# Two of a macro group's last sums move to GpSimd, eleven others and the words of the third product start later

## The chip, the cores and the metric

The kernel runs on one core of one Trainium2 chip, in one launch. The metric is the device time in microseconds, the median of several executions. TensorE is called PE in the profile, VectorE DVE, ScalarE ACT, GpSimd POOL and SyncE SP.

## The reference

The input is a sequence of 2048 rows of 576 numbers. It is normalised row by row; the result goes through a linear-attention block with 32 heads and through a gated feed-forward block, and the two are joined.

```
xn = layernorm(x)
q, k, v = split(xn @ wqkv)                      # 32 heads of 18
s = linear_attention(phi(q), phi(k), v) @ wo
h = gelu(xn @ w_gate) * (xn @ w_up)             # 2048 x 4608
out = x + s * silu(h @ w_down)                  # h @ w_down: 2048 x 576
```

All inputs and outputs are float32.

## The kernel before

Every large product is made in fp32r passes: an operand is cut into a high word (ScalarE copies it to fp32r) and a low word (VectorE subtracts the high word from the source), and TensorE multiplies high by high, high by low and low by high. `split`, `cut` and `make_words` are such pairs of one ScalarE and one VectorE instruction.

The attention part comes first, then 36 matrices of the feed-forward's gate and up projections (`gate_matrix`, `up_matrix`), and last the down projection (`down_all`). The hidden values are kept transposed, 4608 x 2048, and both of these dimensions are split in four, so that one group of values is sixteen blocks of 128 x 512 numbers. Nine such groups (`NM = 9`, called macro groups, m = 0 to 8) make up the whole. The down projection multiplies not the sixteen blocks but fixed sums and differences of them, in 26 products (`PROD`) in place of more. Which sums are needed is written out by hand: `ADDS` lists 28 sums as (name, first operand, second operand, sign, due hook). `ADDS_LAST` is the list for the last macro group. The 26 values that products read (`FORM`) are written to DRAM tensors `hs` (one for each macro group) by `put_out`, 128 x 512 numbers each, and read back for each product by `load_unit`.

**Due hooks.** A matrix has seven hooks, a macro group 28 (`HOOKS`). Hook numbers of group m start at 28 m. `run_events` runs what is due at a hook. For the last group, hooks 0 to 27 lie in the feed-forward, and from hook 28 on in the down projection: there, an event due at hook 28 + n is run in the first step (p, k) in which half the count of contraction tiles done, 9 p + 2 k, has reached n. `add_up` gives a sum to POOL, unless it belongs to the last group and is due after hook 28: then it goes to VectorE. The comparison is

```
late = m == NM - 1 and at > HOOKS * NM
```

so that a last-group sum due at exactly 28 is made by POOL. The same flag says whether a sum may be written over an operand that is still to be put out. The put-outs of the last group are issued on POOL's queue, those of the others on SP's.

**The down projection.** A product p has nine contraction tiles, one for each macro group, taken in five steps k = 0 to 4 (`UNITS`): two tiles in each of the first four, one in the last. A tile is 12 matmuls (four banks, three passes), so a product is 108. In step (p, k) the program order is: the sums that are due; loads of `w_down` (`load_reg`); `change` (VectorE adds and subtracts blocks of `w_down`) or `make_words` (the two words of the next product's weight block: c = 0 is `w_head` or `w_first`, tiles 0 to 4; c = 1 is `w_end`, tiles 5 to 8); `cut(u + 2)`, the cut of the values of the step two further on; the matmuls; the loads of the values of product p + 1 for the same step, into the buffers just read; in step 1 the banks of the product before are read.

Buffers for raw values (`raw_a`, `raw_b`, from product 4 on `raw_h`, `raw_g`) hold the value, and then its low word; `hi` and a part of `beside` hold high words in three places taken in turn. So ScalarE's half of a cut waits until TensorE has finished the step three back, and a load until the buffer is read. Sums and gate values of the last groups live in the buffers `spot_h`, `spot_m` and `spot_g`; `spot_h` becomes `raw_h` later. Products 1 and 23 use the words of the products before them (`SHARED = {1: 0, 23: 22}`), so that in steps 2 and 3 of product 0 the words made are those of product 2.

The engines' instructions are pinned in program order (`tc.keep_in_program_order`); a semaphore wait stops all that follows on the same engine. In the profile every VectorE instruction has line L125, every ScalarE one L122, POOL's sums L131, DMA issues L134, and the down projection's matmuls L128.

Of the kernel before, what the change touches and what calls it, by code (L numbers as in the profile page):

```python
# [62 lines left out]


ADDS_LAST = ADDS[:14] + (
# [4 lines left out]
)  # L70

FORM = (33, 18, 11, 19, 31, 27, 29, 15, 30, 25, 6, 43, 40, 42, 35, 17, 4, 26, 39, 24, 41, 22,
# [18 lines left out]
def block_kernel(ctx, tc, x, xe, wq_d, wkv_d, wo, wgu_d, wd_d, out):  # L91
# [29 lines left out]
    def act(*args, **kw):  # L121
        pin(nc.scalar.activation(*args, **kw))  # L122

    def vec(op, *args, **kw):
        pin(getattr(nc.vector, op)(*args, **kw))  # L125
# [286 lines left out]
    def run(todo, n=None):  # L412
        for _ in range(len(todo) if n is None else min(n, len(todo))):
            todo.pop(0)()
# [438 lines left out]
    def run_events(at):  # L853
        for f in events.pop(at, []):
            f()
# [53 lines left out]
    SHARED = {1: 0, 23: 22}  # L909
    reg, acc_t, banks, raw_v, hi_v, word, early = {}, {}, {}, {}, {}, {}, {}  # L910

    def load_reg(at, nm, third=None):
        if at not in reg:
            b = big(REG[at], [P, REG_W], F32, f"b_{at}")
            reg[at] = b[:, 0 : KT * HALF].rearrange("p (k d) -> p k d", k=KT)
        j, c = int(nm[0]) - 1, int(nm[1]) - 1
        par, f = divmod(KP[j], 2)
        src = wd_d[par::2, :, f, c * HALF : (c + 1) * HALF].rearrange("g p d -> p g d")
        k = slice(0, KT) if third is None else slice(3 * third, 3 * third + 3)
        dma(out=reg[at][:, k], in_=src[:, k])  # L920
# [18 lines left out]
    def load_unit(p, k):  # L939
        if p >= NP:  # L940
            return
        raw_v[p, k] = v = raw_place(p, k)
        for i in range(*UNITS[k]):
            dma(out=v[:, i - UNITS[k][0]].bitcast(F32), in_=hs_d[i][:, PROD[p][0]])
# [13 lines left out]
    def cut(u):  # L958
        p, k = divmod(u, NU)
        if p >= NP:  # L960
            return
        hi, lo = hi_place(p, k), raw_v[p, k]
        hi_v[p, k] = hi
        src = lo.bitcast(F32)
        act(hi, src, AF.Copy)
        vec("tensor_sub", lo, src, hi.bitcast(F32))
# [3 lines left out]
    def word_tiles(p):  # L970
        if p not in word:
            n = len(word)
            b = n % 2
            t = ring(("end", b), lambda: big((11, 4)[b], [P, 2, 4, HALF], F32R, f"w_end{b}"))
            end = [t[:, i] for i in range(2)]
            if b == 0:
                head = [
                    ring(("head", i), lambda i=i: mid(i, [P, 5, HALF], F32R, f"w_head{i}"))
                    for i in (0, 2)
                ]  # L980
            else:
                head = [
                    beside()[:, 2 * TBN : 2 * TBN + 5 * HALF].rearrange("p (k d) -> p k d", k=5),
                    big(12, [P, 5, HALF], F32R, "w_first") if n == 1
                    else ring(("head", 1), lambda: mid(1, [P, 5, HALF], F32R, "w_head1")),
                ]
            word[p] = [[v[i] for v in (head, end)] for i in range(2)]
        return word[p]
# [24 lines left out]
    def change(p, c):  # L1013
        for nm, a, op, b in CHANGES.get(p, ()):
            r = [reg[x][:, HALVES[c]] for x in (nm, a, b)]
            vec("tensor_add" if op == "+" else "tensor_sub", *r)
# [3 lines left out]
    def make_words(p, c):  # L1020

        if p >= NP or p in SHARED or (p, c) in made:
            return
        made.add((p, c))
        hi, lo = (w[c] for w in word_tiles(p))
        src = reg[FROM[p]][:, HALVES[c]]
        if PROD[p][2]:
            act(hi, src, AF.Copy, scale=-1.0)
            vec(
                "scalar_tensor_tensor", lo, src, -1.0, hi.bitcast(F32),  # L1030
                op0=ALU.mult, op1=ALU.subtract,
            )
        else:
            act(hi, src, AF.Copy)
            vec("tensor_sub", lo, src, hi.bitcast(F32))

    def down_mm(p, kt, js):
        if p < 2 and p not in banks:
            banks[p] = [
                (own_bank if p == 0 and i < 2 else bank)(f"bd_{p}_{i}") for i in range(TT)  # L1040
            ]
        c = int(kt > 4)
        hi, lo = (w[c][:, kt - 5 * c] for w in word[SHARED.get(p, p)])
        k = kt // 2
        h = [v[p, k][:, kt % 2] for v in (hi_v, raw_v)]
        for j in js:
            for i, (a, w) in enumerate(((0, hi), (0, lo), (1, hi))):
                mm(
                    banks[p % 2][j][:, 0:HALF], h[a][:, j * P : (j + 1) * P], w,
                    start=(PROD[p][1] == 1 and kt == 0 and i == 0),  # L1050
                    stop=(kt == KT - 1 and i == 2), skip_group_check=True,
                )
# [9 lines left out]
    def read(p, js=range(TT)):  # L1062
        for o, d in PROD[p][3]:
            a = acc_of(o)
            for j in js:
                src = banks[p % 2][j][:, 0:HALF]
                if (o, j) not in begun:
                    begun.add((o, j))
                    act(a[:, j], src, AF.Copy)
                else:  # L1070
                    vec("tensor_add" if d > 0 else "tensor_sub", a[:, j], a[:, j], src)
# [15 lines left out]
    def load_sx(o):  # L1087
        tb, cols, rows = places(o)
        if o in SX:
            sx = big(SX[o], [P, 2, TT, HALF], F32, f"sx_{o}")  # L1090
            all_ = slice(tb * TBN, (tb + 1) * TBN)
            dma(out=sx[:, 0], in_=s_d[tb][:, :, cols])
            dma(out=sx[:, 1], in_=x[all_, cols].rearrange("(t p) d -> p t d", p=P))
            sxs[o] = [sx[:, :, j] for j in range(TT)]
        else:
            sxs[o] = [tmp([P, 2, HALF], f"sx_{o}_{j}") for j in range(TT)]
            for j, t in enumerate(sxs[o]):
                dma(out=t[:, 0], in_=s_d[tb][:, j, cols])
                dma(out=t[:, 1], in_=x[rows(j), cols])
# [3 lines left out]
    def close(o, j):  # L1103
        _, cols, rows = places(o)
        y, t = acc_of(o)[:, j], sxs[o][j]
        act(y, y, AF.Silu, scale=float(SIGN[o]))
        vec("tensor_mul", t[:, 0], y, t[:, 0])
        vec("tensor_add", t[:, 0], t[:, 0], t[:, 1])
        stores.append(lambda: dma(out=out[rows(j), cols], in_=t[:, 0]))
# [40 lines left out]
    def down_all():  # L1150
        late = []
        last = NP - 1
        for u in range(NP * NU):
            p, k = divmod(u, NU)
            n = KT * p + 2 * k
            for at in sorted(events):
                if at <= H_END + n // 2:
                    run_events(at)
            if p in LOADS and k < 3:
                load_reg(*LOADS[p], k)  # L1160
            if k == 0:
                for o, e in ENDS.items():
                    if e == p:
                        load_sx(o)
            if k < 2:
                change(p + 1, k)
            elif k < 4:
                make_words(p + 2 if p + 1 in SHARED else p + 1, k - 2)
            cut(u + 2)
            if p == last and k == 2:  # L1170
                break
            for kt in range(*UNITS[k]):
                down_mm(p, kt, range(TT))
            load_unit(p + 1, k)
            run(stores)
            if k == 1 and p:
                read(p - 1)
                late += [
                    lambda o=o, j=j: close(o, j) for o, e in ENDS.items() if e == p - 1
                    for j in range(TT)  # L1180
                ]
            else:
                run(late, 2)
        run(late)
        run(stores)
        o = next(o for o, e in ENDS.items() if e == last)
        for j in range(TT):
            for kt in range(UNITS[2][0], KT):
                down_mm(last, kt, (j,))
            late += close_last(o, j, last, 2 if j == TT - 1 else 1)  # L1190
            run(late, len(late) - 1)
        run(late)
# [205 lines left out]
    for q in range(NQ):  # L1398
# [9 lines left out]
        for i in range(7):  # L1408
            todo[i].append(lambda at=7 * q + i: run_events(at))
        (gate_matrix if q % 2 == 0 else up_matrix)(g, todo)  # L1410
    down_all()


# [47 lines left out]
```

## Time and profile before

| | |
|---|---|
| median of 3 runs | 1488.77 us (1488.16 to 1489.85) |
| the profiled execution's own time | 1488.81 us |
| its span, first to last instruction | 1487.1 us |
| granted TensorE clock, mean | 0.998 |
| PE / DVE / ACT / POOL busy | 1471.1 / 1145.7 / 560.1 / 581.0 us |
| the down projection's first matmul | at 1103.93 us |

Rows of instructions in order of time read: start in us, length in us, engine, line, operation, output <- input, shape, count, and in brackets the idle time of the engine before it and what ended it. The names are those of the program's tiles without buffer numbers; a sum is a row with `spot_` on both sides, a cut one with `raw_` and `hi` or `beside`. Rows of a table by stretches read: the stretch, its length, the busy time of each engine with its number of instructions, the granted clock, the DMA engines' busy share, and what they moved. PE rows overlap, since matmuls are pipelined.

### The profile page before, as it was taken

The page shows a single profiled execution, that of the slowest core. Times are in us where ns is not written, and L with a number is a line of the kernel's source. Part 1 is how long each engine was busy: PE and PEld are TensorE (multiplying, and loading weights), DVE is VectorE, ACT ScalarE, POOL GpSimd, SP SyncE. Part 2 cuts the span into 40 slices and gives each one's busy share as a digit, 9 for nine tenths or more (in the row PEclk, how much of TensorE's full clock was granted, in tenths as well). Part 3 has the DMA queues.
Part 4 walks back from the last instruction along what each step waited for, and adds up shares of the span by engine and source line. Part 5 has one row for each costly group of instructions (what it writes and reads, how often), then busy time and mean ns, then how long its engine had stood idle before and what let it go on. Part 6 is the DMA issues. An engine that isn't in the chain of part 4 may idle for free.

```text
span 1487.1 us, 21863 instructions
## 1 busy us (share of the span) xinstructions
PE 1471.1 (99%) x8128; PEld 1310.2 (88%) x8128; DVE 1145.7 (77%) x1587; ACT 560.1 (38%) x923; POOL 581.0 (39%) x515
## 2 busy tenths in 40 slices
PE   8999999999999999999999999999999999999998
PEld 8989988988888888888888888888889999999998
DVE  7567466557787788787878787788787988989887
ACT  5434335433223322323322223322234546455454
POOL 4342241124656757555675655757641000000000
PEclk9999999999999999999999999999999999999999
DMA  4425003452231522433242232422379888767886
GB/s 163 176 117 213 6 2 136 167 207 86 92 128 54 181 85 93 149 106 110 82 163 101 98 128 67 167 86 98 129 274 314 262 258 261 240 188 239 272 291 214
DMA packets 115132, 230.62 MB, mean 155 GB/s; under 512 B 10882, under 2 KB 42882, under 8 KB 112978
## 3 DMA queue, kind: packets, MB, share of 16 engines
q1 hardware_dynamic: 112370, 217.17, 43.5%
q0 software_dynamic: 2656, 12.06, 2.2%
q8 instruction: 64, 1.05, 0.3%
q14 instruction: 42, 0.34, 0.1%
HBM read 146.57 MB, written 82.58 MB: 154 GB/s over the span
## 4 chain that ended last, share of the span: by engine, by line
PE 95%; DVE 2%; DMA 1%; issue 1%; ACT 0%; SPq 0%; POOL 0%; DVEq 0%; POOLq 0%; ACTq 0%
PE bd L128 24%; PE ga L746 15%; PE de L746 15%; PE al L746 15%; PE kv L128 8%; PE be L746 7%; PE q L128 4%; PE s L128 4%; PE kv_a L128 1%; PE xt L205 1%; PE d L128 1%; DMA raw<-in_wgu_dram 0%; DVE wb L125 0%; DMA raw_b<-hs 0%; PE kw L128 0%
## 5 line engine op out<-in xcount | busy, mean ns | idle before, releaser
L131 POOL TENSOR_TENSOR sm<-raw 128x384 f32<-128x384 f32 x72 | 76.7, 1065 | 154.6 <-DMA raw<-in_wgu_dram 129.0
L128 PE MATMUL kv<-wkv,xo_B 128*128 128x384 f32 x672 | 127.6, 346 | 0.3 <-ACT xo_B L122 0.3
L125 DVE TENSOR_TENSOR wa<-sm,wa 128x768 fp32r<-128x768 f32 x72 | 93.0, 1291 | 36.1 <-ACT wa L122 35.3
L128 PEld LDWEIGHTS kv<-wkv,xo_B 128*128 128x128 f32 x672 | 119.4, 193 | 1.2 <-ACT xo_B L122 0.8
L128 PE MATMUL bd<-w_head,hi 128*128 128x288 f32 x516 | 118.0, 294 | 0.0
L125 DVE TENSOR_TENSOR wb<-raw,wb 128x256 fp32r<-128x256 f32 (+1 forms) x108 | 108.0, 1000 | 7.3 <-ACT wb L122 5.8
L125 DVE TENSOR_TENSOR wa<-raw,wa 128x256 fp32r<-128x256 f32 x72 | 64.8, 900 | 50.7 <-ACT wa L122 47.5
L122 ACT ACTIVATE hi<-raw_h 128x1024 fp32r<-128x1024 f32 x59 | 62.4, 1060 | 96.8 <-PE bd L128 64.0
L128 PE MATMUL bd<-w_end,hi 128*128 128x288 f32 x448 | 89.9, 294 | 0.0
L122 ACT ACTIVATE spot_h<-spot_h 128x512 f32<-128x512 f32 x49 | 30.8, 633 | 151.7 <-DVE spot_h L125 151.7
L125 DVE TENSOR_TENSOR raw_h<-raw_h,hi 128x1024 fp32r<-128x1024 f32 x59 | 71.7, 1219 | 20.6 <-ACT hi L122 20.5
L128 PEld LDWEIGHTS bd<-w_head,hi 128*128 128x128 f32 x516 | 87.0, 188 | 0.1
L128 PE MATMUL bd<-w_end,raw_h 128*128 128x288 f32 x264 | 77.9, 295 | 0.0
L122 ACT ACTIVATE u<-al 128x512 f32<-128x512 f32 x72 | 41.0, 592 | 90.1 <-PE al L746 81.8
L122 ACT ACTIVATE wa<-sm 128x1152 fp32r<-128x1152 f32 x36 | 41.8, 1161 | 81.6 <-PE de L746 71.0
L128 PEld LDWEIGHTS bd<-w_end,hi 128*128 128x128 f32 x448 | 71.9, 188 | 0.0
L128 PE MATMUL bd<-beside,raw_h 128*128 128x288 f32 x240 | 70.8, 295 | 0.0
L128 PE MATMUL q<-xo_B,wq 128*128 128x512 f32 x240 | 64.1, 395 | 0.0
L746 PE MATMUL ga<-xo_B,wb 128*128 128x512 f32 x252 | 63.3, 390 | 0.4 <-DVE u L125 0.4
L131 POOL TENSOR_TENSOR spot_h<-spot_h,spot_h 128x512 f32<-128x512 f32 x45 | 62.1, 1387 | 2.9 <-DVE spot_h L125 2.4
L746 PE MATMUL al<-xo_B,wa 128*128 128x512 f32 x252 | 63.0, 389 | 0.0
L746 PE MATMUL ga<-xr_B,wb 128*128 128x512 f32 x252 | 63.0, 389 | 0.0
(259 smaller groups left out, 4076.1 us busy)
## 6 DMA issues: line engine op xcount, KB each, us to landing
raw_h<-hs SPq DMA_DIRECT2D x176, 256.0 KB
raw<-in_wgu_dram SPq DMA_DIRECT2D x36, 768.0 KB
hs<-spot_h SPq DMA_DIRECT2D x90, 256.0 KB
hs<-spot_g SPq DMA_DIRECT2D x80, 256.0 KB
b<-in_wd_dram SPq DMA_DIRECT2D x42, 432.0 KB
hs<-spot_m SPq DMA_DIRECT2D x38, 256.0 KB
raw_g<-hs SPq DMA_DIRECT2D x22, 256.0 KB
kept_T<-xo_T SPq DMA_DIRECT2D x4, 1280.0 KB
```

The lines of the kernel that those rows point to most:

```text
L122: pin(nc.scalar.activation(*args, **kw))
L125: pin(getattr(nc.vector, op)(*args, **kw))
L128: pin(nc.tensor.matmul(*args, **kw))
L131: pin(getattr(nc.gpsimd, op)(*args, **kw))
L205: pin(nc.tensor.transpose(xts[n][j][:, k, :], xs[:, j, k * P : (k + 1) * P], ident))
L746: nc.tensor.matmul(o, w[0:rows, wi, :], xop[0:rows, xi, :], start=(start and n == 0), stop=(n == len(PASSES) - 1), skip_group_check=True,)
```

## The change

Two edits.

First, `ADDS_LAST` has other due hooks. Sums 25 and 35 move from hook 29 to hook 28, and are so made by POOL instead of VectorE, behind the sums that it has from the feed-forward's last hooks. As they are no longer late, 35 is written over 25, whose put-out is issued between the two. The eleven sums that VectorE makes move from hooks 30 to 37 to hooks 33 to 41: from steps (0, 2) to (2, 0) to steps (1, 1) to (2, 4). Their put-outs, on POOL's queue, follow them.

Second, the words of product 2 are made in steps 0 and 1 of product 1, behind `change` and ahead of the cut, instead of in steps 2 and 3 of product 0. For the pair 22 and 23 nothing moves: the words of product 24 are still made in steps 2 and 3 of product 22.

```diff
 ADDS_LAST = ADDS[:14] + (
-    (28, 14, 22, 1, 27), (25, 11, 20, 1, 29), (35, 7, 25, -1, 29), (21, 14, 15, 1, 30),
-    (23, 6, 21, 1, 30), (43, 6, 28, 1, 31), (36, 11, 32, -1, 31), (33, 21, 27, 1, 32),
-    (40, 7, 23, 1, 33), (17, 2, 3, 1, 33), (26, 10, 17, 1, 34), (30, 20, 26, -1, 35),
-    (42, 17, 37, -1, 36), (29, 2, 10, 1, 37),
+    (28, 14, 22, 1, 27), (25, 11, 20, 1, 28), (35, 7, 25, -1, 28), (21, 14, 15, 1, 33),
+    (23, 6, 21, 1, 33), (43, 6, 28, 1, 34), (36, 11, 32, -1, 34), (33, 21, 27, 1, 35),
+    (40, 7, 23, 1, 36), (17, 2, 3, 1, 37), (26, 10, 17, 1, 38), (30, 20, 26, -1, 39),
+    (42, 17, 37, -1, 40), (29, 2, 10, 1, 41),
 )
...
             if k < 2:
                 change(p + 1, k)
+                if p in SHARED:
+                    make_words(p + 1, k)
             elif k < 4:
-                make_words(p + 2 if p + 1 in SHARED else p + 1, k - 2)
+                make_words(p + 1, k - 2)
+                if p + 1 in SHARED and p:
+                    make_words(p + 2, k - 2)
             cut(u + 2)
```

Counted by engine, VectorE has two sums less and POOL two more; all else is the same number of instructions in another order.

## The prediction

> **What bounds the kernel now.** I read the page first, then TensorE's waits and the instructions of each engine in order of time around the change, and last the busy time by product. By the page TensorE is busy nearly all of the span, so only what makes it wait can be won.
>
> ```profile
> span 1487.1 us, 21863 instructions
> PE 1471.1 (99%) x8128; PEld 1310.2 (88%) x8128; DVE 1145.7 (77%) x1587; ACT 560.1 (38%) x923; POOL 581.0 (39%) x515
> ```
>
> From the start of the down projection on, TensorE waits three times, each time for VectorE. These are its rows in order of time: the first matmul of products 0, 1, 2 and 3, and between them the three that waited, with the idle time and its releaser in brackets.
>
> ```profile
> 1103.93 0.42 PE L128 MATMUL bd<-w_head,hi 128*128 128x288 f32 x2
> 1115.11 0.40 PE L128 MATMUL bd<-w_end,raw_b 128*128 128x288 f32 x1 [1.24 <-DVE raw_b L125]
> 1119.88 0.40 PE L128 MATMUL bd<-w_end,raw_a 128*128 128x288 f32 x1 [1.33 <-DVE raw_a L125]
> 1121.32 0.42 PE L128 MATMUL bd<-w_head,hi 128*128 128x288 f32 x2
> 1123.49 0.40 PE L128 MATMUL bd<-w_head,raw_a 128*128 128x288 f32 x1 [1.75 <-DVE raw_a L125]
> 1137.62 0.29 PE L128 MATMUL bd<-beside 128*128 128x288 f32 x1
> 1151.92 0.29 PE L128 MATMUL bd<-w_head,hi 128*128 128x288 f32 x1
> ```
>
> The same four starts cut the stretch into products; the columns are length, then busy time of PE, PEld, DVE, ACT, POOL, the clock, the DMA share and GB/s.
>
> ```profile
> 1103.93:1121.32 17.39, 14.82 (x109) 14.35 (x108) 16.02 (x16) 7.00 (x7) 12.47 (x16) 1.00 0.95 344
> 1121.32:1137.62 16.30, 14.55 (x110) 14.32 (x109) 11.89 (x14) 6.10 (x12) 3.99 (x8) 1.00 0.93 311
> 1137.62:1151.92 14.30, 14.30 (x110) 14.30 (x109) 9.99 (x10) 9.25 (x12) 0.54 (x1) 1.00 0.96 313
> 1151.92:1166.22 14.30, 14.30 (x110) 14.30 (x109) 11.96 (x11) 8.20 (x11) 0.00 (x0) 1.00 0.84 292
> ```
>
> An undisturbed product takes 14.30 us. Product 0 is 3.09 over that and product 1 2.00, together 5.09. That is more than the 4.32 of idle time in the three rows, because the pipe also refills after each stop; start-to-start counts what is lost, so 5.09 is the term. VectorE is the late engine: 16.02 of 17.39 us busy in product 0. Here is what it did (VectorE in order of time), with POOL's sums beside it.
>
> ```profile
> 1107.56 1.86 DVE L125 TENSOR_TENSOR raw_b<-raw_b,beside 128x1024 fp32r<-128x1024 f32 x1
> 1109.34 0.68 DVE L125 TENSOR_TENSOR spot_g<-spot_h,spot_g 128x512 f32<-128x512 f32 x1
> 1110.11 2.24 DVE L125 TENSOR_TENSOR spot_g<-spot_m,spot_g 128x512 f32<-128x512 f32 x1
> 1112.27 2.79 DVE L125 TENSOR_TENSOR raw_b<-raw_b,hi 128x1024 fp32r<-128x1024 f32 x1
> 1116.24 0.69 DVE L125 TENSOR_TENSOR spot_g<-spot_g,spot_g 128x512 f32<-128x512 f32 x1 [1.18 <-POOL spot_h L131]
> 1116.96 0.69 DVE L125 TENSOR_TENSOR spot_h<-spot_g,spot_g 128x512 f32<-128x512 f32 x1
> 1117.57 1.65 DVE L125 SCALAR_TENSOR_TENSOR w_first<-b,beside 128x1440 fp32r<-128x1440 f32 x1
> 1119.14 0.68 DVE L125 TENSOR_TENSOR raw_a<-raw_a,hi 128x512 fp32r<-128x512 f32 x1
> 1119.74 0.68 DVE L125 TENSOR_TENSOR spot_h<-spot_g,spot_h 128x512 f32<-128x512 f32 x1
> 1120.35 0.68 DVE L125 TENSOR_TENSOR spot_h<-spot_h,spot_h 128x512 f32<-128x512 f32 x1
> 1120.95 1.35 DVE L125 SCALAR_TENSOR_TENSOR w_end<-b,w_end 128x1152 fp32r<-128x1152 f32 x1
> 1122.22 1.22 DVE L125 TENSOR_TENSOR raw_a<-raw_a,hi 128x1024 fp32r<-128x1024 f32 x1
> ...
> 1110.48 1.31 POOL L131 TENSOR_TENSOR spot_h<-spot_h,spot_m 128x512 f32<-128x512 f32 x1
> 1112.67 1.29 POOL L131 TENSOR_TENSOR spot_h<-spot_m,spot_h 128x512 f32<-128x512 f32 x1
> 1114.84 1.36 POOL L131 TENSOR_TENSOR spot_h<-spot_g,spot_h 128x512 f32<-128x512 f32 x1
> 1116.15 1.09 POOL L134 DMA_DIRECT2D hs<-spot_g  x2
> ```
>
> I write (p,k) for step k of product p. Cut (0,3) is the row at 1112.27: sums 25 and 35 stand ahead of it. Cut (0,4), at 1119.14, stands behind sums 21 and 23, the wait for POOL, and w_first. Cut (1,0), at 1122.22, stands behind sums 43 and 36 and w_end. All of these come off the queue ahead of those three cuts.
>
> A VectorE operation that meets a POOL sum pays for it: 2.24 against 0.68 at 1110.11, and 2.79 against 1.22 at 1112.27, some 1.57 each for POOL sums of 1.31 and 1.29. The Trainium skill ("SBUF — State Buffer", section "SBUF: two separate sides") says that a VectorE operation with two SBUF inputs and a POOL operation exclude each other, and that the one which starts first keeps the port. Here the trace differs in part: VectorE's record began 0.37 us ahead of POOL's, yet VectorE paid.
>
> **The change, part by part.** Spacing of VectorE's starts above: a cut of 1024 occupies 1.14, a cut of 512 0.60, a sum 0.61, w_first 1.57, w_end 1.27.
>
> *Product 0.* These are ScalarE's halves of cuts (0,3) and (1,1):
>
> ```profile
> 1107.17 1.06 ACT L122 ACTIVATE hi<-raw_b 128x1024 fp32r<-128x1024 f32 x1 [3.33 <-PE bd L128]
> 1115.46 1.06 ACT L122 ACTIVATE beside<-raw_a 128x1024 fp32r<-128x1024 f32 x1 [3.40 <-DMA raw_a<-hs]
> ```
>
> After the change cut (0,3) starts at 1109.34, where sum 25 started, its ScalarE half being done at 1108.23, and ends near 1110.5. TensorE wants it at 1103.93 + 6 x 14.30/9 + 0.26 = 1113.7: 3.2 us to spare. Cut (0,4) takes sum 35's place under POOL's sum and ends near 1112.3, wanted at 1116.9. Cut (1,0) takes the place of the row at 1112.27 and ends near 1115.1, wanted at 1118.5. So all three stalls go: 5.09 us, and product 1 starts at 1118.23.
>
> *The two sums on POOL.* They replace two VectorE sums of 0.61, but hold VectorE for about 1.57 each, so the move by itself loads VectorE with 1.9 us more; what helps is that the queue is emptier when it happens. Sum 25 starts near 1116.2, behind the row at 1114.84, and delays cut (1,1) (ready at 1116.5 from ScalarE) to about 1118.8, wanted at 1121.7. Sum 35 is written into 25's buffer, so it waits for 25's put-out to land (this group's put-outs, issue to landing):
>
> ```profile
> DMA to landing us min/median/max: 2.6/4.5/6.2
> ```
>
> 25's put-out goes at about 1117.8, so 35 runs near 1122.3. Behind it in POOL's queue stand only put-outs. Value 35 is first read at (1,4), 1132.5, and 25 far later: no cost on the path.
>
> *Product 1.* VectorE now has, after cut (1,1) at 1118.8: w_first to 1120.4, cut (1,2) to 1121.5 (wanted 1124.8), sums 21 and 23 to 1122.7, w_end to 1124.0, POOL's hold to 1125.6, cut (1,3) to 1126.7, wanted at 1128.0. This is the tightest place: 1.3 us to spare. Then 43, 36 and cut (1,4) to 1128.5 (wanted 1131.2), 33 and cut (2,0) to 1130.3 (wanted 1132.8). The words are wanted only at 1132.5. Cost 0 while these spares last. By that rule of the Trainium skill POOL might wait instead, and the spare at (1,3) would be up to 2.9; the time would be the same.
>
> *Product 2.* Five sums of 0.61 come into a stretch where VectorE now waits:
>
> ```profile
> 1139.68 1.23 DVE L125 TENSOR_TENSOR raw_b<-raw_b,hi 128x1024 fp32r<-128x1024 f32 x1 [1.00 <-ACT hi L122]
> 1142.96 1.23 DVE L125 TENSOR_TENSOR raw_b<-raw_b,beside 128x1024 fp32r<-128x1024 f32 x1 [2.05 <-ACT beside L122]
> ```
>
> 3.05 us fit, as VectorE is busy 9.99 of 14.30. Their put-outs are as large as the page's group of them says:
>
> ```profile
> hs<-spot_h SPq DMA_DIRECT2D x90, 256.0 KB
> ```
>
> Five more of 256 KB in product 2 make 313 GB/s into about 405, where 344 is the most that a product above moved. Excess: 61 GB/s over 14.30 us, 0.87 MB, a backlog of some 2.5 us in the worst case, less what the queue leaves unused (0.04 of 14.30, 0.6). Cut (2,2) at 1139.68 ends at 1140.9 and is wanted at 1137.62 + 6.36 + 0.26 = 1144.2: 3.3 to spare. So again 0 on the path, bounded by 0 and about 1 us.
>
> *Sum.* Profiled execution: 1488.81 = span 1487.1 + 1.7 around it, and the median of the runs is 1488.77. 1488.8 - 5.1 = 1483.7. TensorE waits nowhere later, so nothing gives the gain back unless the whole schedule, moved forward as one, meets something that did not move.
>
> **The rivals.**
> - *VectorE fills product 1.* It has 5.2 of cuts, 2.8 of words, 3.7 of sums and up to 3.1 of POOL's holds, 14.8 against 14.30; only the lead it brings from product 0 covers this. If one more hold falls ahead of cut (1,3), 1.57 - 1.3 to 1.57 us come back: up to 1485.3. Against it: both holds are in the count already. Chance 0.10.
> - *The DMA queue in product 2*, as above with the spare used up: 0.5 to 1.5 back, up to 1485.2. Chance 0.07.
> - *The third stall isn't VectorE's.* The chain of waits leads to it through a load:
>
> ```profile
> 1111.92 5.15 DMA raw_b<-hs
> 1117.57 0.18 DVE w_first L125
> ```
>
> If raw_b's landing decides it, only 3.09 go: 1485.7. Against it: VectorE ran w_first back to back with a sum, so its queue was late by itself. Chance 0.06.
> - *Slower: the last put-out holds the SP queue.* Sum 29 ends the group, and its buffer becomes the raw_h that SP loads first for product 4:
>
> ```profile
> 1139.00 0.54 POOL L134 DMA_DIRECT2D hs<-spot_h  x1 [3.88 <-DVE spot_h L125]
> 1153.02 0.90 SPq L134 DMA_DIRECT2D raw_h<-hs  x2
> 1160.16 1.08 ACT L122 ACTIVATE hi<-raw_h 128x1024 fp32r<-128x1024 f32 x1
> ```
>
> Now 14 us lie between put-out and load. After it, sum 29 stands behind cut (3,0) and its put-out goes near 1146, landing near 1150.5, while SP reaches that load at 1147.9: it and all loads behind it wait 2.6. That is hidden, since ScalarE takes the data only 7.1 us after the issue and TensorE wants them at 1161.1. It decides once the landing is later than about 1153; to come out over 0.2% slower it must be past 1161, through put-outs that wait in POOL's queue: 1492 or more. Chance 0.05.
>
> **How the numbers follow.** Forecast 0.72 at 1483.7; first two rivals 0.17, third 0.06, slower 0.05. A measurement of this kernel tells a change from none at about 0.2%, 3.0 us. "Faster" takes the forecast, the first two and the third, less the part of each that would fall over 1485.8, which I put at 0.11 in all: 0.84. "Same" is this 0.11; slower 0.05. The runs shown lie within 1.1 below to 0.6 above their median, so a median may be off by half a microsecond: the range goes from 1483.0 to 1486.0, up to the second and third rivals.
>
> **What would show it.** Right: no TensorE wait between 1104 and 1150, products 0 to 2 of 14.30 each, cut (0,3) near 1109.3, two POOL sums more, one of them near 1122, VectorE's last sum near 1146. Wrong: a wait on raw_b near 1128 (first rival), on raw_h near 1161 (the slower one), or a product 1 still over 14.30.

## The result, and the profile after

| | before | after |
|---|---|---|
| median of 6 runs each | 1489.02 us (1487.97 to 1489.85) | 1483.26 us (1481.50 to 1483.69) |
| ratio, 95% interval | | 0.9962 (0.9952 to 0.9972) |
| the profiled execution, and its span | 1488.81, 1487.1 us | 1483.02, 1481.3 us |

The changed kernel is faster by 0.38%, 5.8 us. The forecast was 1483.7.

These are the first lines of the page of the changed kernel, then TensorE in order of time, the first matmul of products 0 to 3:

```profile
span 1481.3 us, 21859 instructions
PE 1468.7 (99%) x8128; PEld 1308.9 (88%) x8128; DVE 1141.7 (77%) x1585; ACT 560.3 (38%) x923; POOL 584.5 (39%) x517
...
1103.21 0.42 PE L128 MATMUL bd<-w_head,hi 128*128 128x288 f32 x2
1117.51 0.42 PE L128 MATMUL bd<-w_head,hi 128*128 128x288 f32 x2
1131.81 0.29 PE L128 MATMUL bd<-beside 128*128 128x288 f32 x1
1146.11 0.42 PE L128 MATMUL bd<-w_head,hi 128*128 128x288 f32 x2
```

The table of busy time by product, with the same columns as before (length; PE, PEld, DVE, ACT, POOL; clock, DMA share, GB/s):

```profile
1103.21:1117.51 14.30, 14.30 (x110) 14.30 (x109) 12.74 (x10) 5.42 (x6) 12.30 (x14) 1.00 0.99 350
1117.51:1131.81 14.30, 14.30 (x111) 14.30 (x110) 12.99 (x14) 7.68 (x14) 4.84 (x8) 1.00 0.97 329
1131.81:1146.11 14.30, 14.30 (x111) 14.30 (x110) 11.04 (x13) 8.20 (x11) 2.58 (x5) 1.00 1.02 372
1146.11:1160.41 14.30, 14.30 (x111) 14.30 (x110) 13.00 (x12) 9.26 (x12) 0.13 (x1) 1.00 0.93 323
```

Each of these four products now takes 14.30 us, and no matmul in them waits. Later in the down projection TensorE waits once, 0.10 us at 1318.23; the kernel before has the same wait at 1324.05. From the first matmul of product 0 to the end of the span there were 1487.1 - 1103.93 = 383.17 us; now there are 1481.3 - 1103.21 = 378.09. The difference is 5.08, where the prediction's term was 5.09. The other 0.7 of the 5.8 between the two spans lies ahead of product 0, where both kernels run the same instructions; in the nine profiles of this study that first matmul comes between 1103.01 and 1104.49, so 0.7 there is not the change's.

VectorE and POOL around the stops that went, in order of time:

```profile
1108.62 1.22 DVE L125 TENSOR_TENSOR raw_b<-raw_b,hi 128x1024 fp32r<-128x1024 f32 x1
1109.76 4.59 DVE L125 TENSOR_TENSOR raw_a<-raw_a,hi 128x512 fp32r<-128x512 f32 x2
1115.83 2.00 DVE L125 TENSOR_TENSOR raw_a<-raw_a,beside 128x1024 fp32r<-128x1024 f32 x1 [1.49 <-ACT beside L122]
1117.76 1.65 DVE L125 SCALAR_TENSOR_TENSOR w_first<-b,beside 128x1440 fp32r<-128x1440 f32 x1
1119.32 1.21 DVE L125 TENSOR_TENSOR raw_b<-raw_b,hi 128x1024 fp32r<-128x1024 f32 x1
1120.46 2.50 DVE L125 TENSOR_TENSOR spot_g<-spot_g,spot_g 128x512 f32<-128x512 f32 x2
1122.88 1.35 DVE L125 SCALAR_TENSOR_TENSOR w_end<-b,w_end 128x1152 fp32r<-128x1152 f32 x1
1124.15 1.22 DVE L125 TENSOR_TENSOR raw_b<-raw_b,hi 128x1024 fp32r<-128x1024 f32 x1
...
1115.45 1.30 POOL L131 TENSOR_TENSOR spot_g<-spot_h,spot_g 128x512 f32<-128x512 f32 x1
1120.18 1.50 POOL L131 TENSOR_TENSOR spot_g<-spot_m,spot_g 128x512 f32<-128x512 f32 x1 [2.58 <-DMA hs<-spot_g]
1145.70 0.54 POOL L134 DMA_DIRECT2D hs<-spot_h  x1 [2.20 <-DVE spot_h L125]
```

Cut (0,3) starts at 1108.62, 5.41 us after product 0, where sum 25 started before. Cuts (0,4) and (1,0) follow at once (one row, x2) and end at 1114.35; TensorE wants (1,0) at 1117.8. Sums 25 and 35 stand in POOL's rows, and the 2.58 in brackets is 35 waiting for 25's put-out. Of the cuts that the change moves, the tightest is (1,3), at 1124.15: it ends at 1125.37 and is wanted at 1117.51 + 9.53 + 0.26 = 1127.30, so it has 1.9 us to spare. (Cut (0,2), the first row of VectorE that the prediction shows, has less, 1.1, with and without the change.)

### The profile page after: what moved, and what is told of

It is laid out like the page before. It is cut to its first block, busy times and chain, and to the rows that moved or that the text cites. A ratio compares the mean times of both kernels' runs of the same rounds, so it can differ in the third digit from the quotient of the medians.

```text
span 1481.3 us, 21859 instructions
## 1 busy us (share of the span) xinstructions
PE 1468.7 (99%) x8128; PEld 1308.9 (88%) x8128; DVE 1141.7 (77%) x1585; ACT 560.3 (38%) x923; POOL 584.5 (39%) x517
## 4 chain that ended last, share of the span: by engine, by line
PE 95%; DVE 2%; POOL 1%; DMA 1%; issue 1%; ACT 0%; DVEq 0%; POOLq 0%; SPq 0%; ACTq 0%
PE bd L128 24%; PE ga L746 15%; PE de L746 15%; PE al L746 14%; PE kv L128 8%; PE be L746 7%; PE q L128 4%; PE s L128 4%; PE kv_a L128 1%; PE xt L205 1%; PE d L128 1%; DMA hs<-spot_g 0%; DVE wa L125 0%; POOL spot_h L131 0%; PE kw L128 0%
## 5 line engine op out<-in xcount | busy, mean ns | idle before, releaser
L746 PE MATMUL al<-xr_B,wa 128*128 128x512 f32 x252 | 63.0, 389 | 0.0
```

What stands on the lines that cost most here:

```text
L746: nc.tensor.matmul(o, w[0:rows, wi, :], xop[0:rows, xi, :], start=(start and n == 0), stop=(n == len(PASSES) - 1), skip_group_check=True,)
```

## The experiments

In all of them "loss" is the time from the first matmul of product 0 to that of product 2, less 28.60 (two products of 14.30). It is 5.09 before and 0 after.

### The words alone, and the sums alone

The first run moves the words and keeps `ADDS_LAST` as before; the second has the new `ADDS_LAST` and the old place of the words.

```diff
 # words alone: of the change, only this
             if k < 2:
                 change(p + 1, k)
+                if p in SHARED:
+                    make_words(p + 1, k)
             elif k < 4:
-                make_words(p + 2 if p + 1 in SHARED else p + 1, k - 2)
+                make_words(p + 1, k - 2)
...
 # sums alone: of the change, only this
 ADDS_LAST = ADDS[:14] + (
+    (28, 14, 22, 1, 27), (25, 11, 20, 1, 28), (35, 7, 25, -1, 28), (21, 14, 15, 1, 33),
...
```

Expected of the words alone:

> The words of product 2 move, all thirteen sums stay where they were. If VectorE's queue ahead of each cut decides the stops (the prediction's theory): cut (0,3) stays behind sums 25 and 35 and stops TensorE as before (1.5 us lost); cut (0,4) is freed of w_first and comes at about 1118.2 where TensorE wants it, no stop; cut (1,0) is freed of w_end and ends near 1120.5, wanted at 1120.0, about 0.8 lost. Loss over three undisturbed products 2.3 instead of 5.1, time about 1485.6. Rival, that the words are worth nothing because the sums fill the same time: loss 5.1, time 1488.8. Rival, that the words are the whole: loss 0, time 1483.3.

Expected of the sums alone:

> Two sums on POOL and eleven deferred, the words of product 2 stay in product 0. By VectorE's queue: cut (0,3) ends near 1110.5, no stop; w_first under POOL's holds to about 1114, cut (0,4) near 1115, no stop (wanted 1116.9); w_end under POOL's 28 and the new 25 to 1118 or 1119, cut (1,0) to 1119 or 1120, wanted 1118.5: one stop, loss 0.5 to 1.9, time 1483.8 to 1485.2. Rival, that the words are what counts: two stops of 3.5 remain, 1486.8.

Measured: words alone 1485.53, ratio 0.9973 (0.9964 to 0.9983); sums alone 1486.26, ratio 0.9982 (0.9973 to 0.9990). TensorE's waits in the profile of the words alone, in order of time:

```profile
1115.28 0.40 PE L128 MATMUL bd<-w_end,raw_b 128*128 128x288 f32 x1 [2.02 <-DVE raw_b L125]
1120.83 0.40 PE L128 MATMUL bd<-w_head,raw_a 128*128 128x288 f32 x1 [0.48 <-DVE raw_a L125]
```

And of the sums alone, with VectorE and POOL ahead of the wait:

```profile
1119.63 0.40 PE L128 MATMUL bd<-w_head,raw_a 128*128 128x288 f32 x1 [1.67 <-DVE raw_a L125]
...
1109.79 2.84 DVE L125 SCALAR_TENSOR_TENSOR w_first<-b,beside 128x1440 fp32r<-128x1440 f32 x1
1112.55 1.78 DVE L125 TENSOR_TENSOR raw_a<-raw_a,hi 128x512 fp32r<-128x512 f32 x1
1114.25 4.19 DVE L125 SCALAR_TENSOR_TENSOR w_end<-b,w_end 128x1152 fp32r<-128x1152 f32 x1
...
1111.98 1.80 POOL L131 TENSOR_TENSOR spot_h<-spot_m,spot_h 128x512 f32<-128x512 f32 x1
1114.65 1.31 POOL L131 TENSOR_TENSOR spot_h<-spot_g,spot_h 128x512 f32<-128x512 f32 x1
1115.90 1.31 POOL L131 TENSOR_TENSOR spot_g<-spot_h,spot_g 128x512 f32<-128x512 f32 x1
```

The stops are where the queue ahead of each cut puts them: the words free (0,4) and most of (1,0) and leave (0,3); the sums free (0,3) and (0,4) and leave (1,0). The losses are 3.04 and 1.94 (expected 2.3, and 0.5 to 1.9). The words alone lost more at (0,3) because VectorE stood 0.8 us later against TensorE in that execution: its cut (0,3) starts 9.12 us after product 0, against 8.34 before.

The median of the sums alone, 1486.26, missed the range expected, 1483.8 to 1485.2, and lies nearer to the 1486.8 of the rival. The profile shows one stop and not that rival's two, but the profiled execution (1484.99) is the second fastest of twelve (1484.79 to 1489.61), and what the others lost is open. Neither half is the whole. In the profiles the words save 2.1 of the 5.1 and the sums 3.2; by the medians, against 1489.22 for the kernel before, it is 3.7 and 3.0. So which half is worth more is not shown.

### Two sums to POOL, and nothing else

```diff
 ADDS_LAST = ADDS[:14] + (
-    (28, 14, 22, 1, 27), (25, 11, 20, 1, 29), (35, 7, 25, -1, 29), ...
+    (28, 14, 22, 1, 27), (25, 11, 20, 1, 28), (35, 7, 25, -1, 28), ...
```

> Only sums 25 and 35 go to POOL; the other eleven sums and the words stay as before. By VectorE's queue with a hold of 1.57 for each POOL sum: cut (0,3) is free, but sum 21 still waits for POOL to 1116.2, then sum 25 on POOL holds it, cut (0,4) ends near 1121 (wanted 1116.9) and cut (1,0) near 1126 with the hold of sum 35: loss about 8, time about 1491, slower than before by 2. Rival, that moving sums to POOL relieves VectorE by 0.61 each: loss 5.1 - 1.2 = 3.9 or less, time 1487.2 or less.

Measured: 1490.99, ratio 1.0013 (1.0004 to 1.0021), loss 7.2. Slower than before, as expected, but the clock has a part in it. Of the 7.2 in the profile, the two stops are 5.8 from start to start; the other 1.4 is TensorE at half clock behind the first. The seven runs with a mean granted clock of 0.994 to 0.996 took 1490.60 to 1493.22, the four with 0.998 only 1488.29 to 1489.99, against 1489.22 for the kernel before. TensorE's waits, VectorE's row behind its own wait, and the table of two short stretches (columns as above, the clock third from last):

```profile
1120.29 0.61 PE L128 MATMUL bd<-w_end,raw_a 128*128 128x288 f32 x1 [3.85 <-DVE raw_a L125]
1124.99 0.40 PE L128 MATMUL bd<-w_head,raw_a 128*128 128x288 f32 x1 [1.52 <-DVE raw_a L125]
...
1115.58 2.49 DVE L125 TENSOR_TENSOR spot_g<-spot_g,spot_g 128x512 f32<-128x512 f32 x2 [5.62 <-POOL spot_h L131]
...
1116.00:1120.00 4.00, 0.44 (x4) 0.21 (x2) 3.97 (x4) 1.72 (x2) 1.34 (x2) 0.98 0.75 288
1120.00:1122.00 2.00, 1.71 (x7) 1.71 (x8) 2.00 (x3) 0.00 (x0) 1.65 (x1) 0.50 0.00 0
```

VectorE finishes cut (0,3) early and then stands 5.62 us for POOL, since sum 21 overwrites a buffer that POOL's last sum reads. Relieving an engine of two sums is worth nothing while its next instruction in order waits.

### All thirteen sums on VectorE, with the new and with the old words

```diff
-... (25, 11, 20, 1, 28), (35, 7, 25, -1, 28), ...
+... (25, 11, 20, 1, 33), (35, 7, 25, -1, 33), ...
```

With the words as in the changed kernel:

> All thirteen sums on VectorE, 25 and 35 deferred to step (1,1) with 21 and 23; words as in the changed kernel. If the deferral is what counts and not POOL: no stop, loss 0, time 1483.3, and cut (1,3) does not come later than in the changed kernel, since 1.2 us of sums replace up to 3.1 of holds. Rival, that the move to POOL is needed: cut (1,3) misses, loss 1 or more, time 1484.3 or more.

With the words as before:

> Thirteen sums on VectorE, deferred (25 and 35 to step (1,1)), and the words of product 2 stay in product 0: the fourth corner beside the changed kernel, the run with sums alone and the run with all on VectorE. If sum 25 on POOL is what made w_end 4.19 long in the run with sums alone, w_end now meets only one POOL sum: 2.8 long, cut (1,0) ends near 1118.2 for a TensorE that wants it at 1117.8, loss 0.3 to 0.7, time about 1483.8 against 1485.2 to 1486.3 there. Rival, that the words in product 0 cost the same with or without the move to POOL: loss 1.9, time 1485.3.

Measured: 1483.39, ratio 0.9959 (0.9947 to 0.9971), loss 0, no wait; and with the old words 1483.92, ratio 0.9964 (0.9951 to 0.9976), loss 0.68. First VectorE's cut (1,3) with the new words; then TensorE's wait and VectorE's w_end with the old ones:

```profile
1125.05 1.22 DVE L125 TENSOR_TENSOR raw_b<-raw_b,hi 128x1024 fp32r<-128x1024 f32 x1
```

```profile
1118.39 0.40 PE L128 MATMUL bd<-w_head,raw_a 128*128 128x288 f32 x1 [0.41 <-DVE raw_a L125]
...
1114.26 2.94 DVE L125 SCALAR_TENSOR_TENSOR w_end<-b,w_end 128x1152 fp32r<-128x1152 f32 x1
```

So the four corners of loss, all with the eleven sums deferred:

| | words moved | words as before |
|---|---|---|
| 25 and 35 on POOL | 0 (the changed kernel) | 1.94 |
| 25 and 35 on VectorE, deferred | 0 | 0.68 |

The move to POOL gains nothing in either column. In the right one it costs 1.26: w_end meets two POOL sums in a row and takes 4.19, against 2.94 with one. The lower right corner also shows that deferring the thirteen sums is nearly the whole of the gain, 4.41 of the 5.09, where nothing goes to POOL; moving the words as well then adds 0.68, which the timed runs (ratios 0.9964 and 0.9959, with intervals that overlap) cannot tell from nothing. The expectation for cut (1,3) was missed by a little: it ends 22.49 us after product 0 against 22.16 in the changed kernel. VectorE waited 0.64 longer for ScalarE ahead of cut (1,1) there, and the holds that went were smaller than assumed (below).

### Seven sums in one step

```diff
-... (43, 6, 28, 1, 34), (36, 11, 32, -1, 34), (33, 21, 27, 1, 35), (40, 7, 23, 1, 36), (17, 2, 3, 1, 37), ...
+... (43, 6, 28, 1, 33), (36, 11, 32, -1, 33), (33, 21, 27, 1, 33), (40, 7, 23, 1, 33), (17, 2, 3, 1, 33), ...
```

> As the changed kernel, but seven of the eleven sums (21, 23, 43, 36, 33, 40, 17) are all due in step (1,1), ahead of w_end and cut (1,3). That is five sums more there, 3.05 us. If the spare at cut (1,3) is real and bounded, TensorE stops there and only there: the changed kernel's profile shows 2.0 us to spare, so 3.05 - 2.0 and some refill, 1.0 to 1.3 lost, time about 1484.5 (by the prediction's spare of 1.3: 2.0 lost, 1485.3). Rival, that VectorE has slack to give everywhere in product 1: loss 0, 1483.3.

Measured: 1484.69, ratio 0.9972 (0.9961 to 0.9983), loss 1.12, in one stop:

```profile
1129.60 0.40 PE L128 MATMUL bd<-w_end,raw_b 128*128 128x288 f32 x1 [0.86 <-DVE raw_b L125]
```

The spare at cut (1,3) is real, and about 1.9: five more sums, 3.05 us, overran it by about 1.

### All thirteen sums on POOL

All the late sums are due at hook 28, so that VectorE makes none.

```diff
-... (21, 14, 15, 1, 33), (23, 6, 21, 1, 33), ... (42, 17, 37, -1, 40), (29, 2, 10, 1, 41),
+... (21, 14, 15, 1, 28), (23, 6, 21, 1, 28), ... (42, 17, 37, -1, 28), (29, 2, 10, 1, 28),
```

> All thirteen sums go to POOL at hook 28, none to VectorE; words as in the changed kernel. POOL needs some 2.2 us for a sum and its put-out and waits where it writes over a value that is still being put out: some 34 us, from 1115 to 1149. If a POOL sum holds VectorE's operations by up to 1.57, VectorE carries in product 1 up to 10 us of holds beside 8 of its own, more than 14.30 less its lead, and the last put-out lands after 1153, so that SP waits for it before the loads of product 4: loss 1 to 4, time 1484.5 to 1487.5, stops in product 1 or 2 or near the first step of product 4. Rival, that POOL is free help: loss 0, 1483.3.

Measured: 1484.74, ratio 0.9974 (0.9963 to 0.9984). TensorE waits once, at the start of product 3; VectorE's row before it, and the short stretches behind it:

```profile
1148.81 0.61 PE L128 MATMUL bd<-w_head,raw_a 128*128 128x288 f32 x1 [2.47 <-DVE raw_a L125]
...
1146.47 4.74 DVE L125 TENSOR_TENSOR raw_a<-raw_a,hi 128x1024 fp32r<-128x1024 f32 x2
...
1148.00:1150.00 2.00, 1.19 (x5) 1.19 (x6) 2.00 (x2) 0.09 (x1) 1.74 (x2) 0.62 1.02 339
1150.00:1152.00 2.00, 2.00 (x10) 2.00 (x10) 2.00 (x2) 0.00 (x0) 0.67 (x2) 0.53 0.92 281
```

Two cuts that take 2.35 before take 4.74 here. The median is in the range expected, but the stop comes a product later than "product 1 or 2", since sum 35 began only at 1123 behind 25's put-out. Product 3 is 4.11 us longer here: 2.64 by the stop, start to start, and 1.47 by the half clock behind it. This profiled execution (1487.16) was the slowest of its seven runs; whether the others had a smaller stop or kept the clock is not shown.

## Why the prediction was right

*The term.* 5.09 us of lost time in products 0 and 1, all of it from VectorE's queue: 5.08 came back. Counting start to start and not the 4.32 of idle time was needed for that. The spans differ by 0.7 more, which lies ahead of product 0; so it is the 5.08, and not the median (1483.26 for a forecast of 1483.7), that bears the term out.

*Product 0.* The three cuts come at the places worked out, within 0.1 us against the product's start: cut (0,3) at 5.41 after it (forecast 5.41), cut (1,0) done at 11.14 (11.17).

*Product 1.* Here a size was off. Each POOL sum was put at 1.57 of VectorE's time; in the changed kernel 25 cost cut (1,1) 2.00 - 1.22 = 0.78, and 35 cost sums 21 and 23 about 1.1 (2.50 against the 1.41 from 1116.24 to 1117.65 before). 35 itself took 1.50 where POOL's other sums there take 1.30 to 1.43, so POOL seems to have paid a part. Sum 35 also came 1.4 earlier against the product's start than forecast, its predecessor's put-out having landed after some 3 us and not 4.5. The spare at cut (1,3) was 1.9, not 1.3. None of this changed the time.

*The DMA queue in product 2.* Forecast 405 GB/s at worst; measured 372 at a share of 1.02. The queue was full, yet no matmul waited. Here is ScalarE's half of cut (2,2):

```profile
1133.71 1.06 ACT L122 ACTIVATE hi<-raw_b 128x1024 fp32r<-128x1024 f32 x1 [2.96 <-DMA raw_b<-hs]
```

VectorE's half ended at 1136.0 and was wanted at 1131.81 + 6.36 + 0.26 = 1138.4: 2.4 to spare, 0.9 less than before.

*The rivals.* "VectorE fills product 1" did not happen here; seven sums in one step show that it does once the 1.9 us are overrun. "The third stall isn't VectorE's" is refuted: raw_b's four loads are issued 6.9 to 9.2 us after product 0, before 6.9 to 8.7, so no earlier; with the queue cleared ScalarE cuts raw_b (first row below) without any wait for a load, and TensorE does not stop. The step to the load in the chain of waits was an inference of the view, not a cause. In the slower rival one link was wrong: SP did not stop at the first loads of raw_h.

```profile
1116.99 1.04 ACT L122 ACTIVATE hi<-raw_b 128x1024 fp32r<-128x1024 f32 x1
...
1147.29 1.01 SPq L134 DMA_DIRECT2D raw_h<-hs  x2
1148.90 1.34 SPq L134 DMA_DIRECT2D raw_h<-hs  x2
```

They went out at 1147.29, 1.6 us after the last put-out was issued; the second pair took 1.34, 0.5 longer than the 0.84 it took before. In the trace the put-out landed at 1149.63 and the fourth load was issued then; the queue's own waits put 0.7 us down to that put-out, and none before. So the buffer of sum 29 is not the first one needed, and the forecast wait of 2.6 came out as 0.5 to 0.7, hidden.

*The spread of the runs.* The prediction has it the wrong way round: 1488.16 to 1489.85 about 1488.77 is 0.6 below and 1.1 above. The half microsecond that it takes for the median is the same either way.

## What to carry to other kernels

Where an engine works through a fixed order, look at what stands ahead of the late instruction, not at the engine's load: 5 us came from moving work that nobody needed yet behind work that was due, and handing two pieces to a helper engine added nothing. Before deferring, write down for each step when its result is wanted and how much is spare; the tightest spare that the change touched was 1.9 us, and one step with five more sums used it up. Count a stop from start to start, and keep stops short: behind the two longest here the clock fell too.

## What the runs showed of the hardware that was not expected

*A stop can cost the clock as well.* After the stops of 3.85 us (two sums to POOL) and 2.47 us (all on POOL) the granted clock fell to 0.50 and 0.53 in the rows above, and the first matmul took 0.61 in place of 0.40. It stayed low for 3.4 us each time, which cost some 1.4 us on top of the stop. After 2.02 us (the words alone) and 1.75 us (before) it stayed at 1.00. The Trainium skill ("TensorE: Matmul & The Clock Gate", section "Part 1: The HAM clock gate (the "warmup" mystery)") puts the fall behind an idle window of about 3.4 us; here a stop of 2.47 was enough in one execution.

*The hold between VectorE and POOL goes both ways.* With the sums alone, a POOL sum that began 2.2 us into w_first took 1.80 against 1.31, and in the changed kernel sum 35 began 0.86 us into a cut and took 1.50; in the kernel before, VectorE's operations that began 0.4 us ahead of POOL paid all of it. The rule of the Trainium skill that the prediction tells ("SBUF — State Buffer", section "SBUF: two separate sides"), that the one which starts first keeps the port, fits the first two cases and not the last; what decides in the first half microsecond stays open.
